# A list scheduler's cost table is rewritten, with a resource shared by VectorE and GpSimd

## The chip, the core and the metric

The program runs on one core of a Trainium2 chip. The metric is the device time of one execution in microseconds. TensorE multiplies matrices, VectorE (DVE in the profile), ScalarE (ACT) and GpSimd (POOL) do the elementwise work, and SyncE (SP) issues the DMAs. SBUF is the on-chip memory of all of them; PSUM holds TensorE's results and is not read by GpSimd.

## What is computed

Banded attention with a few sink columns, and behind it two feed-forward layers without residuals, all in float32. Shapes: 4 batch elements, 8 heads, 768 positions, 64 per head; 3072 tokens, d_model 512, d_ff 2048.

```
scores = scale * q @ k^T;  keep = (pos_k < n_sink) | (0 <= pos_q - pos_k < window)   # 4 and 128
a = softmax(where(keep, scores, -1e9)) ; x = (a @ v) as (tokens, 512)
h = relu(x @ w_in);      x = (h * h) @ w_out            # first layer
h = x @ w2_in;           y = (h - tanh(h)) @ w2_out     # second layer
```

The weights arrive as float64 words.

## The kernel before

Every float32 operand of a product is split into a high part, rounded to the type that TensorE multiplies fast, and a low part, the rest; a product is three fast ones (high by high, high by low, low by high). A split is a copy that rounds, on ScalarE or VectorE (`copy`, L200), and a subtraction, on VectorE or GpSimd (`sub`, L211). The subtraction reads two tensors in SBUF.

The work has these parts. Attention runs by jobs, a head's half of the queries, eight to a block of 384 tokens (`scores` L258, `values` L350; the jobs of blocks 0 and 1 are `plain`, L390, in float32 products without splits). Each weight half-chunk of 512 columns is loaded and turned from float64 to a high and a low float32 part (`w_split`, L485): a rescaling on ScalarE or VectorE (L500, L502), a shift (L509) and two bit merges (L511, L513) on VectorE, a rounding copy, a subtraction. The first layer (`step1`, L546) goes over 8 blocks of 384 tokens and 16 chunks of d_ff: a product into the PSUM bank `ph` (L527), relu (L557), square (L563), split, and the product into four accumulating banks (L541). The second (`step2`, L578) goes over 6 blocks of 512 tokens with a longer elementwise chain (L583 to L596) and two banks, `ph` and `S`, in turns, and accumulates at L543. The second layer's 32 weight halves take the places of the first layer's as these come free in its last block; `y_in` (L608) reads the first layer's result back from memory.

The order of the instructions is not written by hand. Each operation is added with the engines that may run it and a duration on each (`add`, L83), a due time by which operations are ranked, and the buffers that it reads and writes. `solve` (L102) then walks through model time. It takes the engine that is free first, goes through the operations ready on it, most urgent first, and gives it the first one that no other engine permitted for it would end earlier:

```
if all(max(free[g], op.ready.get(g, 0.0)) + queue(g, item) + op.engs[g] * self.WEIGH[g] >= now + op.engs[e] * self.WEIGH[e]
       for g in op.engs if g != e):
```

`queue` is the model time of the more urgent operations that are ready on the other engine, each divided by the number of engines that may run it. `WEIGH` counts VectorE's durations twice. The table `HOP` holds the wait from an operation's end to the start of one that needs it, by pairs of engines. The durations come from `c_act`, `c_dve`, `c_copy`, `c_sub` and `c_mm` (L168 to L186). At the end the operations are emitted in the order of their model starts; on the chip every engine runs its own in that order, and waits at the head of its queue for what the next one needs.

Of the kernel before, what the change touches and what calls it, by code (L numbers as in the profile page):

```python
# [38 lines left out]
PLAIN = 2 * H          # jobs (a head's half of the queries) in float32 products, those of the first batch element  # L39
# [4 lines left out]
# h - tanh(h) where u = h^2 < 1/64: h u (c0 + c1 u + c2 u^2) = h u ((s u + b)^2 + d), to float32's accuracy  # L44
# [17 lines left out]
# ---------------------------------------------------------------- order of the instructions  # L62
class Op:
    __slots__ = ("engs", "prio", "emit", "left", "out", "ready", "start", "eng", "lat")


class Order:
    """Places operations on the engines: what is ready, most urgent first, on the engine that ends it first.

    Operations are added in an order that is right when run one after the other; what one has to wait for  # L70
    follows from the buffers that it reads and writes."""

    # from an operation's end on one engine to the start of one on another that waits for it
    HOP = {"TV": 200.0, "TA": 200.0, "AV": 131.0, "VV": 127.0, "PV": 180.0, "VA": 128.0, "AA": 143.0, "PA": 169.0, "AP": 165.0, "VP": 155.0,
           "PP": 75.0, "AT": 217.0, "VT": 256.0, "PT": 200.0, "TP": 200.0, "VD": 500.0, "AD": 500.0, "TD": 500.0, "PD": 500.0}
    AHEAD = {"V": 900.0, "D": 1050.0}
    TICK, FIRST = 3413.0, 4590.0
    WEIGH = {"V": 2.0, "A": 1.0, "P": 1.0}
# [4 lines left out]
    def add(self, engs, prio, reads, writes, emit, lat=0.0):  # L83
        op = Op()
        op.engs, op.prio, op.emit, op.left, op.out, op.ready, op.eng, op.lat = engs, prio, emit, 0, [], {}, None, lat
# [15 lines left out]

    def solve(self):  # L102
# [3 lines left out]
        tick = {int(self.FIRST // self.TICK): self.TICK}  # L106

# [8 lines left out]
        def queue(g, item):  # L116
            return sum(i[2].engs[g] / len(i[2].engs) for i in avail[g] if i < item and i[2].eng is None)

        def cost(op, e, now):
            c = op.engs[e]  # L120
            if e == "T":    # TensorE's clock is halved after a tick in which it had little to do
                n = int((self.FIRST + now) // self.TICK)
                t = c if tick.get(n - 1, 0.0) >= 0.375 * self.TICK else 2.0 * c
                tick[n] = tick.get(n, 0.0) + c
                return t
            return c

        done, n = [], len(self.ops)
        while len(done) < n:
# [6 lines left out]
            best, skipped = None, []  # L136
# [18 lines left out]
            best.eng, best.start = e, now  # L155
            free[e] = now + cost(best, e, now)
            done.append(best)
            for d in best.out:
                for g in d.engs:
                    d.ready[g] = max(d.ready.get(g, 0.0), free[e] + self.HOP.get(e + g, 0.0) + best.lat)  # L160
# [4 lines left out]
        return max(free.values())  # L165
# [12 lines left out]


def c_sub(n):  # L180
    return {"V": c_dve(n), "P": 2.1 * n + 150}


def c_mm(n):
    return n / 2.4 + 1


class Fast:
    """The banded path, 0 <= n_sink <= 4 and 1 <= window <= 128: each query's window is one block of 128 columns,
    the later keys of the block before it and the earlier ones of its own, and 4 sink columns."""  # L190
# [8 lines left out]
    # one operation each; get() gives its operands when it is placed  # L199
# [11 lines left out]
    def sub(self, prio, reads, writes, get, n):  # L211
# [5 lines left out]
        self.o.add(c_sub(n), prio, reads, writes, emit)  # L217

    def load(self, prio, writes, get, nbytes, reads=()):
# [796 lines left out]
```

## Time and profile before

| | |
|---|---|
| device time, median of 3 runs | 1319.19 us (1318.81 to 1319.56) |
| span of the profiled execution | 1319.0 us |
| TensorE busy | 1267.7 us, 96% |
| VectorE busy | 1043.0 us, 79%, 2227 instructions |
| ScalarE busy | 749.8 us, 57%, 1909 instructions |
| GpSimd busy | 393.1 us, 30%, 511 instructions |

The span reaches from the program's first instruction to its last, and the profile page gives no other time for that execution; it lies within the range of the runs. TensorE's busy time counts pipelined matmuls whose ends are modelled, so its share overstates it. A wait at TensorE is booked either at the matmul (PE) or at the load of its weights (PEld).

### The profile page before, as it was taken

To read this page: it belongs to the slowest core of one execution; us is meant where nothing else is said; L and a number is where in the kernel's file an instruction comes from. 1 tells how busy PE (TensorE), PEld (TensorE's weight loads), DVE (VectorE), ACT (ScalarE), POOL (GpSimd) and SP (SyncE) were. 2 spreads that over 40 slices of the span, in tenths; PEclk is the share of its full clock that TensorE was granted. 3 is DMA by queue.
4 is the path that set the end of the run, shared out by engine and by line. 5 is a ranking of instruction groups with operands and counts; after the bars stand their busy time and mean duration, and the time that the engine had idled before them with its cause. 6 is when DMAs were issued, how large, how long until landed. Compare 5 with 4: busy or idle time off the path is not lost. (4 is left out here: it accounts for less than half of the span.)

```text
span 1319.0 us, 19532 instructions
## 1 busy us (share of the span) xinstructions
PE 1267.7 (96%) x6696; PEld 1120.9 (85%) x6696; DVE 1043.0 (79%) x2227; ACT 749.8 (57%) x1909; POOL 393.1 (30%) x511
## 2 busy tenths in 40 slices
PE   8889899999999999999998899999999999999998
PEld 5578799999999999999998777788888888888886
DVE  6899977888787888778848999886777776777665
ACT  5666566766677666776655555454444444544443
POOL 3466344455433555334534544100000000000000
PEclk9999999999999999999999999999999999999999
DMA  7773112221222212112018740010100100000000
GB/s 231 257 257 132 50 60 80 70 70 50 73 63 66 83 50 67 58 59 82 29 41 284 226 143 1 1 65 0 33 32 1 56 8 1 33 0 0 33 0 35
DMA packets 41723, 94.99 MB, mean 72 GB/s; under 512 B 4752, under 2 KB 18576, under 8 KB 41616
## 3 DMA queue, kind: packets, MB, share of 16 engines
q1 hardware_dynamic: 41472, 93.27, 21.7%
q8 instruction: 54, 0.88, 0.3%
q14 instruction: 53, 0.43, 0.1%
q10 hardware_dynamic: 144, 0.40, 0.1%
HBM read 79.50 MB, written 14.16 MB: 71 GB/s over the span
## 5 line engine op out<-in xcount | busy, mean ns | idle before, releaser
L527 PE MATMUL ph<-xh,w 128*128 128x384 f32 x1024 | 296.9, 341 | 8.7 <-ACT r L557 6.2
L541 PE MATMUL acc<-gh,w 128*128 128x384 f32 x1024 | 301.6, 345 | 0.3 <-ACT y L206 0.2
L543 PE MATMUL acc<-w,g2h 128*128 128x512 f32 x768 | 258.5, 396 | 0.0
L527 PEld LDWEIGHTS ph<-xh,w 128*128 128x128 f32 x1024 | 188.8, 189 | 13.9 <-ACT r L557 9.4
L541 PEld LDWEIGHTS acc<-gh,w 128*128 128x128 f32 x1024 | 188.3, 188 | 2.2 <-issue 0.9
L541 PE MATMUL acc<-gl,w 128*128 128x384 f32 x512 | 175.0, 342 | 7.4 <-DVE gl L216 3.9
L527 PE MATMUL ph<-xl,w 128*128 128x384 f32 x512 | 173.1, 338 | 2.0 <-DVE xl L216 1.8
L543 PEld LDWEIGHTS acc<-w,g2h 128*128 128x128 f32 x768 | 144.6, 188 | 34.0
L206 ACT CAST g2h<-r 128x512 fp32r<-128x512 f32 x94 | 58.3, 620 | 201.9 <-DVE r L596 201.8
L543 PE MATMUL acc<-w,g2l 128*128 128x512 f32 x384 | 152.6, 397 | 2.1 <-DVE g2l L216 1.1
L330 POOL TENSOR_SCALAR_AFFINE_SELECT pt<-xe 128x256 fp32r<-128x256 f32 (+1 forms) x192 | 92.8, 508 | 132.8 <-ACT xe L206 122.9
L527 PE MATMUL ph<-x2h,w 128*128 128x512 f32 x384 | 128.8, 394 | 3.3 <-DVE w L594 3.1
L527 PE MATMUL S<-x2h,w 128*128 128x512 f32 x384 | 127.8, 391 | 0.4 <-DVE w L594 0.4
L216 DVE TENSOR_TENSOR g2l<-r,g2h 128x512 fp32r<-128x512 f32 x90 | 62.2, 691 | 60.8 <-ACT g2h L206 60.8
L541 PEld LDWEIGHTS acc<-gl,w 128*128 128x128 f32 x512 | 96.2, 188 | 14.1 <-POOL gl L216 7.8
L284 ACT ACTIVATE cb<-cb,nm 128x132 f32<-128x132 f32 x144 | 58.6, 407 | 78.8 <-DVE nm L341 78.6
L216 POOL TENSOR_TENSOR x2l<-raw,x2h 128x512 fp32r<-128x512 f32 x12 | 17.4, 1449 | 285.3 <-ACT x2h L206 176.5
L527 PEld LDWEIGHTS ph<-xl,w 128*128 128x128 f32 x512 | 96.8, 189 | 4.0 <-DVE xl L216 3.7
L543 PEld LDWEIGHTS acc<-w,g2l 128*128 128x128 f32 x384 | 72.3, 188 | 21.3 <-DVE g2l L216 2.3
L527 PEld LDWEIGHTS ph<-x2h,w 128*128 128x128 f32 x384 | 72.6, 189 | 20.7 <-DVE w L594 3.9
L557 ACT ACTIVATE r<-ph 128x384 f32<-128x384 f32 x128 | 62.5, 488 | 46.2 <-PE ph L527 44.4
L590 DVE TENSOR_SCALAR mk<-u 128x512 uint8<-128x512 f32 x96 | 45.3, 472 | 54.3 <-ACT u L583 54.3
(189 smaller groups left out, 2768.3 us busy)
## 6 DMA issues: line engine op xcount, KB each, us to landing
wr<-w SPq DMA_DIRECT2D x64, 512.0 KB, 5.1
raw<-raw SPq DMA_DIRECT2D x32, 454.0 KB, 3.3
raw<-raw SPq DMA_DIRECT2D x31, 388.0 KB, 3.1
yd<-y SPq DMA_DIRECT2D x40, 192.0 KB, 2.5
raw<-yd SPq DMA_DIRECT2D x28, 256.0 KB, 2.9
out<-y SPq DMA_DIRECT2D x20, 256.0 KB, 2.0
raw<-raw SPq DMA_DIRECT2D x24, 160.0 KB, 2.9
raw<-raw SPq DMA_DIRECT2D x24, 128.0 KB, 2.2
```

Of the source, the lines that this page charges most:

```text
L206: nc.scalar.copy(out=out, in_=in_)
L216: (nc.vector if e == "V" else nc.gpsimd).tensor_tensor(out=out, in0=a, in1=b.bitcast(F32), op=ALU.subtract)
L284: lambda e, i=i: nc.scalar.activation(out=t[cb][:, i, :], in_=t[cb][:, i, :], func=AF.Exp, bias=t[nm][:, i:i + 1], scale=-1.0, accum_out=t ...
L330: lambda e, u=u, n=n, s=s, sign=sign, op=op: nc.gpsimd.affine_select(out=slots(u, n, s), in_=t[xe][:, 2 * u:2 * (u + n), :], pattern=[[0, ...
L527: nc.tensor.matmul(out=ph[:, :N], lhsT=w[:, a + c * P:a + (c + 1) * P], rhs=b[:, c, :], start=(c == 0 and k == 0), stop=(c == NE - 1 and k ...
L541: nc.tensor.matmul(out=acc[:, :N1], lhsT=w[:, a + e_ * P:a + (e_ + 1) * P], rhs=g, start=st, stop=sp)
L543: nc.tensor.matmul(out=acc, lhsT=g[:, e_ * P:(e_ + 1) * P], rhs=w[:, a:a + 512], start=st, stop=sp)
L557: nc.scalar.activation(out=r, in_=ph, func=AF.Relu)
L590: lambda e: nc.vector.tensor_scalar(out=T[mk], in0=T[u], scalar1=U_MAX, scalar2=None, op0=ALU.is_lt))
```

## The change

No instruction is added or removed; operations may go to another permitted engine or to another place in the order. Due times stay as they are. Comments are removed.

A duration becomes a triple `C(occ, took, port)`: how long the engine is occupied, how long until the result is there, and whether the operation needs the resource that VectorE and GpSimd share. All of GpSimd's operations need it, and of VectorE's those on SBUF alone; those that read PSUM don't. The weight of 2 on VectorE goes. The hops shrink, since they now count from `took`. Where the engine is ready earlier than the shared resource, the operation is held, and one of lower urgency may go first if it ends in time.

```diff
-    HOP = {"TV": 200.0, "TA": 200.0, "AV": 131.0, "VV": 127.0, "PV": 180.0, "VA": 128.0, "AA": 143.0, "PA": 169.0, "AP": 165.0, "VP": 155.0,
-           "PP": 75.0, "AT": 217.0, "VT": 256.0, "PT": 200.0, "TP": 200.0, "VD": 500.0, "AD": 500.0, "TD": 500.0, "PD": 500.0}
-    AHEAD = {"V": 900.0, "D": 1050.0}
+    HOP = {"TV": 40.0, "TA": 45.0, "AV": 35.0, "VV": 35.0, "PV": 40.0, "VA": 40.0, "AA": 35.0, "PA": 36.0, "AP": 75.0, "VP": 95.0,
+           "PP": 350.0, "AT": 55.0, "VT": 56.0, "PT": 56.0, "TP": 60.0, "TT": -160.0}
+    AHEAD = {"V": 1100.0, "D": 400.0}
-    WEIGH = {"V": 2.0, "A": 1.0, "P": 1.0}
+    NEAR = 60.0
...
+        def begin(op, e, now):
+            return max(now, port - 60.0) if op.engs[e][2] else now
...
-                if all(max(free[g], op.ready.get(g, 0.0)) + queue(g, item) + op.engs[g] * self.WEIGH[g] >= now + op.engs[e] * self.WEIGH[e]
+                at = begin(op, e, now)
+                if all(max(free[g], op.ready.get(g, 0.0), port if op.engs[g][2] else 0.0) + queue(g, item) + op.engs[g][1] >= at + op.engs[e][1]
                        for g in op.engs if g != e):
-                    best = op
-                    break
+                    if at <= now + self.NEAR:
+                        if held is None or now + op.engs[e][0] <= held[0] + self.NEAR:
+                            best = op
+                            break
+                    elif held is None:
+                        held = (at, item)
+                        continue
                 skipped.append(item)
...
+            if best.engs[e][2]:
+                port = max(port, at + occ)
...
 def c_act(n, psum=False, ptr=0):
-    return n / 1.2 + (51 if psum else 93) + 93 * ptr
-def c_dve(n, fast=False, ptr=0):
-    return n / (1.92 if fast else 0.96) + 70 + 60 * ptr
+    return C(n / 1.2 + (48 if psum else 98) + 92 * ptr, n / 1.2 + (162 if psum else 194) + 92 * ptr)
+def c_one(n, psum=False):
+    return C(n / 0.96 + 70) if psum else C(n / 1.92 + 70, None, True)      # None: took = occ + 85
+def c_two(n, psum=False):
+    return C(n / 0.96 + 72, None, not psum)
 def c_copy(n, psum=False):
-    return {"A": c_act(n, psum), "V": c_dve(n, not psum)}
-def c_sub(n):
-    return {"V": c_dve(n), "P": 2.1 * n + 150}
-def c_mm(n):
-    return n / 2.4 + 1
+    return {"A": c_act(n, psum), "V": c_one(n, psum)}
+def c_pool(n):
+    return C(2.35 * n + 110, 2.35 * n + 115, True)
+def c_sel(n):
+    return C(0.89 * n + 130, 0.89 * n + 180, True)
+def c_mm(*ns, slow=1):
+    t = sum(slow * (n * 0.4355 + 6.0) for n in ns)
+    return C(t, t + 165.0)
...
-        self.o.add({"D": max(nbytes / 360.0, 480.0)}, prio, reads, writes, emit, lat=2200.0)
+        t = max(nbytes / 300.0, 430.0)
+        self.o.add({"D": C(t, t + 1700.0)}, prio, reads, writes, emit)
```

A subtraction's durations are now `c_two` on VectorE and `c_pool` on GpSimd; the rescaling of weights costs ScalarE `c_act(568)`; the normalization of a job costs GpSimd 950 ns; the row minimum costs VectorE 222 ns and 375 ns to its result; the float32 products of `plain` take `slow=1.85`.

## Rows read from the trace of the kernel before

**Rows 1.** Page, busy tenths of two engines in 40 slices of the span

```profile
PE   8889899999999999999998899999999999999998
DVE  6899977888787888778848999886777776777665
```

**Rows 2.** Windows: bounds and length, each engine's busy time (instructions), clock, DMA

```profile
0.00:30.00 30.00, 24.33 (x101) 15.35 (x102) 19.50 (x100) 16.57 (x67) 10.66 (x26) 1.00 0.70 230
30.00:180.00 150.00, 131.40 (x715) 111.33 (x714) 142.02 (x318) 94.77 (x272) 77.47 (x81) 0.98 0.50 165
180.00:690.00 510.00, 504.88 (x3208) 497.33 (x3208) 396.54 (x1085) 343.26 (x1049) 230.81 (x353) 1.00 0.20 61
690.00:840.00 150.00, 133.85 (x633) 112.70 (x632) 142.92 (x202) 79.80 (x146) 62.84 (x43) 0.99 0.45 149
840.00:1319.00 479.00, 473.22 (x2048) 384.16 (x2046) 342.04 (x526) 215.40 (x377) 11.32 (x8) 1.00 0.06 21
```

**Rows 3.** Windows, the same columns (PE PEld DVE ACT POOL), two shorter stretches

```profile
60.00:150.00 90.00, 79.95 (x443) 68.73 (x444) 88.17 (x181) 55.17 (x147) 48.43 (x48) 1.00 0.51 172
720.00:840.00 120.00, 107.04 (x486) 87.78 (x487) 118.09 (x168) 63.17 (x115) 52.75 (x36) 0.99 0.34 113
```

**Rows 4.** Waits of PEld, 30 to 180 us: total, times, longest

```profile
PEld S L409 <- DVE pcb L417: 7.1, 9, 1.5
PEld O L471 <- POOL ppp L464: 6.6, 6, 2.5
```

**Rows 5.** Waits of PEld, 690 to 840 us

```profile
PEld ph L527 <- ACT r L557: 8.8, 10, 2.0
```

**Rows 6.** Timeline of VectorE near 740 us: start, duration, instruction

```profile
739.41 1.50 DVE L216 TENSOR_TENSOR w<-wd,w 128x512 fp32r<-128x512 f32 x1
740.84 1.78 DVE L513 SCALAR_TENSOR_TENSOR wd<-wr,wd 128x512 int32<-128x512 int32 x1
742.55 0.41 DVE L509 TENSOR_SCALAR wd<-wd 128x512 int32<-128x512 int32 x1
```

**Rows 7.** Timeline of GpSimd in the same stretch

```profile
738.98 1.40 POOL L216 TENSOR_TENSOR gl<-r,gh 128x384 fp32r<-128x384 f32 x1 [3.01 <-DVE gh L208]
740.33 1.74 POOL L216 TENSOR_TENSOR x2l<-raw,x2h 128x512 fp32r<-128x512 f32 x1
```

**Rows 8.** Source view of single lines, whole run: duration ns least/median/most

```profile
L513 DVE SCALAR_TENSOR_TENSOR wd<-wr,wd x64: 654/688/1782, 24.3 to 836.3; 128x512 int32<-128x512 int32 x64
L216 DVE TENSOR_TENSOR w<-wd,w x26: 677/692/1667, 46.4 to 837.7; 128x512 fp32r<-128x512 f32 x26
L216 DVE TENSOR_TENSOR gl<-r,gh x97: 535/558/1524, 61.2 to 747.4; 128x384 fp32r<-128x384 f32 x97
```

**Rows 9.** Lines by form, VectorE, 690 to 840 us: busy us, mean ns

```profile
L513 DVE SCALAR_TENSOR_TENSOR wd<-wr,wd 128x512 int32<-128x512 int32 x32 | 31.3, 977 | 0.4
L208 DVE CAST g2h<-r 128x512 fp32r<-128x512 f32 x2 | 2.0, 978 | 0.1
```

**Rows 10.** Lines by form, VectorE, 30 to 180 us

```profile
L513 DVE SCALAR_TENSOR_TENSOR wd<-wr,wd 128x512 int32<-128x512 int32 x31 | 27.5, 896 | 0.1
L441 DVE TENSOR_TENSOR psk<-pcb,prs 128x12 f32<-128x12 f32 x4 | 1.6, 406 | 0.0
```

**Rows 11.** Windows of line 216 (subtractions) alone: VectorE busy, GpSimd busy

```profile
30.00:180.00 150.00, 25.17 (x33) 50.13 (x38) 0.98 0.50 165
690.00:840.00 150.00, 23.34 (x28) 56.39 (x38) 0.99 0.45 149
```

**Rows 12.** Lines by form, ScalarE, 690 to 840 us; last column idle before, releaser

```profile
L500 ACT ACTIVATE wd<-wr 128x512 f32<-128x512 f32 x27 | 18.2, 676 | 24.4 <-DVE w L216 13.1 <-POOL w L216 8.3 <-DMA wr<-w 2.7
L206 ACT CAST w<-wd 128x512 fp32r<-128x512 f32 x27 | 16.6, 617 | 22.7 <-DVE wd L513 22.6
```

**Rows 13.** Timeline of VectorE near 868 us, GpSimd idle

```profile
868.48 0.69 DVE L216 TENSOR_TENSOR g2l<-r,g2h 128x512 fp32r<-128x512 f32 x1 [0.74 <-ACT g2h L206]
869.09 0.42 DVE L590 TENSOR_SCALAR mk<-u 128x512 uint8<-128x512 f32 x1
```

More of the change, by code (lines that the diff above doesn't have):

```diff
@@ L63, with __new__, times, add @@
 class Op:
-    __slots__ = ("engs", "prio", "emit", "left", "out", "ready", "start", "eng", "lat")
+    __slots__ = ("engs", "prio", "emit", "left", "out", "ready", "start", "eng", "end")
+class C(tuple):
+    def __new__(cls, occ, took=None, port=False):
+        return tuple.__new__(cls, (occ, occ + 85.0 if took is None else took, port))
+    def times(self, k):
+        return C(self[0] * k, self[0] * (k - 1) + self[1], self[2])
 class Order:
-    HOP = {"TV": 200.0, "TA": 200.0, "AV": 131.0, "VV": 127.0, "PV": 180.0, "VA": 128.0, "AA": 143.0, "PA": 169.0, "AP": 165.0, "VP": 155.0,
-           "PP": 75.0, "AT": 217.0, "VT": 256.0, "PT": 200.0, "TP": 200.0, "VD": 500.0, "AD": 500.0, "TD": 500.0, "PD": 500.0}
-    AHEAD = {"V": 900.0, "D": 1050.0}
+    HOP = {"TV": 40.0, "TA": 45.0, "AV": 35.0, "VV": 35.0, "PV": 40.0, "VA": 40.0, "AA": 35.0, "PA": 36.0, "AP": 75.0, "VP": 95.0,
+           "PP": 350.0, "AT": 55.0, "VT": 56.0, "PT": 56.0, "TP": 60.0, "TT": -160.0}
+    AHEAD = {"V": 1100.0, "D": 400.0}
     TICK, FIRST = 3413.0, 4590.0
-    WEIGH = {"V": 2.0, "A": 1.0, "P": 1.0}
+    NEAR = 60.0
     def __init__(self):
         self.ops, self.writer, self.readers = [], {}, {}
-    def add(self, engs, prio, reads, writes, emit, lat=0.0):
+    def add(self, engs, prio, reads, writes, emit):
         op = Op()
-        op.engs, op.prio, op.emit, op.left, op.out, op.ready, op.eng, op.lat = engs, prio, emit, 0, [], {}, None, lat
+        op.engs, op.prio, op.emit, op.left, op.out, op.ready, op.eng = engs, prio, emit, 0, [], {}, None
         deps = set()
@@ L116, in queue @@
         def queue(g, item):
-            return sum(i[2].engs[g] / len(i[2].engs) for i in avail[g] if i < item and i[2].eng is None)
+            return sum(i[2].engs[g][0] / len(i[2].engs) for i in avail[g] if i < item and i[2].eng is None)
         def cost(op, e, now):
@@ L135, in solve @@
                     heapq.heappush(avail[e], (op.prio, r, op))
-            best, skipped = None, []
+            best, held, skipped = None, None, []
             while avail[e]:
@@ L154, in solve @@
                 continue
-            best.eng, best.start = e, now
-            free[e] = now + cost(best, e, now)
+            at = begin(best, e, now)
+            occ, took = cost(best, e, at)
+            best.eng, best.start, best.end = e, at, at + took
+            free[e] = at + occ
+            if best.engs[e][2]:
+                port = max(port, at + occ)
             done.append(best)
@@ L159, in solve @@
                 for g in d.engs:
-                    d.ready[g] = max(d.ready.get(g, 0.0), free[e] + self.HOP.get(e + g, 0.0) + best.lat)
+                    d.ready[g] = max(d.ready.get(g, 0.0), best.end + self.hop(e, g))
                 d.left -= 1
@@ L286, in scores @@
         d = due[2]
-        o.add({"V": 73.0}, d - 9.9, [(*ss, i) for i in range(3)], [ss],
+        o.add({"V": c_one(3)}, d - 9.9, [(*ss, i) for i in range(3)], [ss],
               lambda e: nc.vector.tensor_scalar(out=t[ss], in0=t[ss], scalar1=1e-9, scalar2=None, op0=ALU.add))
-        o.add({"V": 80.0}, d - 9.8, [ss], [rs] + [(*ss, i) for i in range(3)], lambda e: nc.vector.reciprocal(out=t[rs], in_=t[ss]))
+        o.add({"V": C(95)}, d - 9.8, [ss], [rs] + [(*ss, i) for i in range(3)], lambda e: nc.vector.reciprocal(out=t[rs], in_=t[ss]))
         def norm(e):
@@ L328, in scores @@
             for s, sign, op in ((1, 1, ALU.is_ge), (0, -1, ALU.is_gt)):
-                o.add({"P": 0.91 * 2 * P * n + 128}, d - 5, [xk], [("pt", 2 * i + s) for i in range(u, u + n)],
+                o.add({"P": c_sel(2 * P * n)}, d - 5, [xk], [("pt", 2 * i + s) for i in range(u, u + n)],
                       lambda e, u=u, n=n, s=s, sign=sign, op=op: nc.gpsimd.affine_select(
@@ L339, in least @@
         m = self.c["m"][0 if half == 0 and i == 0 else 1 if half == 0 and i == 1 else 2]
-        self.o.add({"V": c_dve(132) + 8}, prio, [cb], [cb] + out,
+        self.o.add({"V": C(222, 375, True)}, prio, [cb], [cb] + out,
                    lambda e: nc.vector.tensor_tensor_reduce(out=get(), in0=get(), in1=m, op0=ALU.add, op1=ALU.min, scale=scale,
@@ L366, in pv @@
             nc.tensor.matmul(out=oo[:, :N1], lhsT=vv[:, 0, :], rhs=pts, start=False, stop=True)
-        o.add({"T": c_mm(N1) + (5 + 2 * half) * c_mm(256)}, d - 4,
+        o.add({"T": c_mm(N1, *[256] * (5 + 2 * half))}, d - 4,
               [("vh", k2), ("vl", k2)] + [("pts", k2, i) for i in range(3)] + [("pt", s) for s in range(1 - half, 6)], [ob], pv)
@@ L429, in plain @@
         d = due[2]
-        o.add({"V": 73.0}, d - 9.9, [(*ss, i) for i in range(3)], [ss],
+        o.add({"V": c_one(3)}, d - 9.9, [(*ss, i) for i in range(3)], [ss],
               lambda e: nc.vector.tensor_scalar(out=t[ss], in0=t[ss], scalar1=1e-9, scalar2=None, op0=ALU.add))
-        o.add({"V": 80.0}, d - 9.8, [ss], [rs] + [(*ss, i) for i in range(3)], lambda e: nc.vector.reciprocal(out=t[rs], in_=t[ss]))
+        o.add({"V": C(95)}, d - 9.8, [ss], [rs] + [(*ss, i) for i in range(3)], lambda e: nc.vector.reciprocal(out=t[rs], in_=t[ss]))
         def norm(w, out):
@@ L442, in norm @@
             return emit
-        o.add({"A": 3 * c_act(P, ptr=1), "V": c_dve(N1), "P": 2.1 * N1 + 150}, d - 9, [rs] + cbs, cbs, norm(slice(SK, 132), lambda: t[cb][:, :, SK:]))
-        o.add({"V": c_dve(3 * SK), "P": 2.1 * 3 * SK + 150}, d - 9, [rs] + cbs, [psk],
+        o.add({"A": c_act(P, ptr=1).times(3), "V": c_two(N1), "P": C(830, None, True)}, d - 9, [rs] + cbs, cbs, norm(slice(SK, 132), lambda: t[cb][:, :, SK:]))
+        o.add({"V": c_two(3 * SK), "P": C(260, None, True)}, d - 9, [rs] + cbs, [psk],
               norm(slice(0, SK), lambda: t[psk].rearrange("p (n s) -> p n s", s=32)[:, :, :SK]))
@@ L451, in tr @@
             nc.tensor.transpose(out=tt[0:96, 3 * P:4 * P], in_=t[psk], identity=self.c["idf"])
-        o.add({"T": 440.0}, d - 7, cbs + [psk], [tb], tr)
+        o.add({"T": c_mm(P, P, P, P, slow=1.75)}, d - 7, cbs + [psk], [tb], tr)
         if i0:
@@ L473, in pv @@
                 nc.tensor.matmul(out=out[:, i * P:(i + 1) * P], lhsT=v[0:96, (i - 1) % 3, :], rhs=t[ps][0:96, :], start=False, stop=(i == 2))
-        o.add({"T": 1000.0}, d - 4, [("rv", q), ps] + [(*pp, i) for i in range(3)], [ob], pv)
+        o.add({"T": c_mm(*[256] * (5 + 2 * half - 2 + half), *[P] * 6, slow=1.85)}, d - 4, [("rv", q), ps] + [(*pp, i) for i in range(3)], [ob], pv)
         self.copy(d - 3, [ob], [(*x, r)], lambda: (t[x][r:r + 64], bank[ob][r:r + 64, :N1]), N1, True)
```

78 lines of the change are left out of this document (44 added, 34 removed).

## The prediction

> **What bounds the kernel now.** Read the page's slices first: TensorE stands at 9 nearly everywhere, but dips at both ends of a long plateau, and just there VectorE stands at 8 and 9 [rows 1]. The windows by stage put numbers on it [rows 2]. From 180 to 690 us TensorE is busy 505 of 510 us, and from 840 on 473 of 479, the missing 6 lying behind the last product; no order of the elementwise work can win much there. From 30 to 180 and from 690 to 840, where weights are converted, it idles 18.6 and 16.2 us, and VectorE is busy 142.0 and 142.9 of 150. In the cores of these stages VectorE has no room left: 88.2 of 90 us and 118.1 of 120 [rows 3]. So two stages, 300 us together, are bound by VectorE, and the waits of TensorE's loads say through whom: in the first the masked scores of `plain` and GpSimd's selects come late [rows 4], in the second relu, which frees the bank `ph` [rows 5].
>
> But VectorE's busy time there isn't all work. At 739.41 a subtraction that alone takes 0.69 us (median, [rows 8]) took 1.50, ending 0.53 us after GpSimd's subtraction ended at 740.38; the merge behind it took 1.78 beside GpSimd's next one, and the shift after that is at its usual 0.41 [rows 6, 7]. Busy time of VectorE is here time spent held by GpSimd, and GpSimd's 1.40 and 1.74 are in part the reverse. The change's new resource describes that.
>
> The profiled span is 1319.0 us and the median 1319.19; I take the 0.2 us between them as what lies around the span and sum from 1319.2.
>
> **The change, part by part.** Nothing is added or removed, so each part is priced by which operations it sends elsewhere.
>
> *Subtractions from GpSimd to VectorE.* Before, a 512-wide one counted 2 x 603 = 1207 ns on VectorE and 1225 on GpSimd: GpSimd got it as soon as VectorE's backlog was 19 ns longer than its own. Now it counts 690 and 1318, and since the shared resource delays both alike, VectorE keeps it up to a backlog of some 630 ns (384 wide: 460). That is a strong push off GpSimd. What one is worth: in 690 to 840 us thirteen of VectorE's forms run above their undisturbed medians, the first L513 with 32 x (977 - 688) ns = 9.2 us, the last the rounding of g2h with 1.1 [rows 8, 9]; together 34 us, beside 62.8 us of GpSimd's work, so 0.54 us of VectorE for each us of it. In 30 to 180 us sixteen forms, first L513 with 31 x (896 - 688) ns = 6.4 us, last the small scaling of psk with 1.0 [rows 8, 10], give 40 us beside 77.5, so 0.51. A subtraction on GpSimd takes 56.39/38 = 1.48 us in the later stage and 50.13/38 = 1.32 in the earlier [rows 11]; it costs VectorE 0.80 and 0.67 us. On VectorE it costs its median less the 0.08 us by which the next instruction starts before its end [rows 13]: 0.61 us for 512 columns, 0.47 for 384 [rows 8], on average 0.57 and 0.54 with the widths of each stage. So a moved one gains 0.23 and 0.13 us, and all 76 of them 8.7 + 4.9 = 13.6. With a queue always standing at VectorE the planner will still pass the 630 ns often; I take half: **-7 us**. From both sides: L513 alone gives 9.2/38 = 0.24 us held per subtraction, by which a moved one loses 0.33 and half of them 13 us; the two of [rows 6] lost (1.50 - 0.69) + (1.78 - 0.69) = 1.90, so 0.95 each, by which all 76 gain 30. I stand by the sums over all forms, since they hold all of the excess.
>
> The trace and the Trainium skill differ on the 0.08 us. "VectorE: DVE Perf Modes", section "The DRAIN you can't avoid", says that the next VectorE instruction doesn't start until the pipe of the one before is empty; a later section of the page lets an instruction that isn't held start earlier. By the first, a moved subtraction would cost its full 0.69 us, half of them would gain 3 us less, and the table's `occ` would be 85 ns short on every VectorE instruction. Here 868.48 + 0.69 = 869.17, and the next one starts at 869.09 [rows 13], so I keep the overlap.
>
> *Roundings from ScalarE to VectorE.* The weight of 2 held these off VectorE: 673 ns against ScalarE's 520. Now 422 stand against 621, and for the rescaling of weights 422 against 667, so VectorE takes one up to a backlog of 199 or 245 ns. It has far more than that where it is bound, which limits the harm, but ScalarE is idle there for 24.4 and 22.7 us before these very operations, waiting for VectorE's chain [rows 12], and at such moments the backlog can be short. Each costs VectorE about its shift's 0.41 less 0.08, 0.33 us. There are 54 of the two kinds on ScalarE in 690 to 840 us [rows 12], and I take nine of those and of the earlier stage's: **+3 us**. Ends: a result 0.2 us earlier at each of nine links of the chain gains 2; all 54 lose 18, and with no more than as many in the earlier stage 36.
>
> *Durations to the result, hops, and holding.* In the model GpSimd's work now delays VectorE as it does on the chip, so a relu is less often queued on ScalarE behind a rounding whose input is late. The waits on this are 8.8 us at `ph`, and 6.6 and 7.1 at the selects and scores [rows 4, 5]: 22.5 us. I take a quarter, as part goes with the first term: **-5.5 us**; ends: none gained and as many lost again as taken, or all 22.5.
>
> *TensorE's and the DMAs' figures, the heads' start.* A 384-wide product counts 173 instead of 161 ns, loads 430 to 1748 instead of 480 to 1456. TensorE's and SyncE's own order follows the due times, which don't change; DMA is at half its share or less in these stages [rows 2]. Zero, hidden by the plateau of TensorE; the first 30 us, where TensorE idles 5.7, can move 2 either way. In 180 to 690 us GpSimd's normalizations also lean to VectorE, at 397 of 510 us; TensorE's 5 idle us there are the most to be won, and I give the plateau 0, plus or minus 5.
>
> Sum: 1319.2 - 7 + 3 - 5.5 = 1309.7, rounded to **1310 us**.
>
> **Rivals.** *Roundings swamp VectorE.* If the planner sends most of the roundings and rescalings over, say 72 of the 108 at most, VectorE gets 72 x 0.33 = 24 us in stages where it is the chain, against 12.5 gained: 1319 + 11 = **1330**. It decides from about 38 moved. For: a preference turned round by some 350 ns, and VectorE already full. Against: its backlog is counted before each choice. Chance 0.22.
>
> *No net change.* In a standing queue GpSimd keeps its subtractions, since 630 ns is one waiting merge, and what is gained by holding is lost again elsewhere: **1319**, within 2.6. For: 98% busy means that a queue is nearly always there. Against: the model now books VectorE as held, so it plans with less idle time. Chance 0.13.
>
> *The waits nearly vanish.* With all of the 13.6 us and two thirds of the 22.5, and three us of roundings: 1319.2 - 13.6 - 15 + 3 = **1294**. For: nothing but order stands behind those waits. Against: a greedy planner doesn't look ahead. Chance 0.13.
>
> *VectorE's instructions don't overlap.* If each holds the engine for its full duration, 38 moved subtractions cost 38 x 0.08 = 3 us more: **1313**. The start at 869.09 speaks against it [rows 13]. Chance 0.02. (It is the first of the two sections of the Trainium skill's page weighed above that would have it so.)
>
> **Numbers.** The forecast has 0.50, with its own range 1300 to 1316. About 0.2%, 2.6 us, is what a measurement of this kernel can tell from no change. Faster: 0.50 + 0.13 + 0.02 = 0.65, less 0.02 for a forecast that ends short of 2.6 us; same 0.13 + 0.02; slower 0.22. The range is 1290 to 1327: the lower end lies past the case of vanishing waits, the upper takes in the rounding case up to some 60 moved, and leaves out its worst.
>
> **What would show it.** Right: GpSimd's line 216 falls from 38 instructions in each of the two stages to about 19; L513's mean falls from 977 and 896 towards 690; VectorE stays near full in both stages, which end some 4 to 8 us earlier each; relu's wait at `ph` falls below 7; from 840 us on nothing changes but its start. Wrong: ScalarE's roundings and rescalings falling by more than a third there, with VectorE at 150 of 150; GpSimd's count unchanged; or new waits of TensorE between 180 and 690 us beyond 5.

## The result, and the profile after

The changed kernel takes 1297.99 us (median of 4 runs, 1297.06 to 1300.17) beside 1319.38 for the kernel before on the same chip: ratio 0.9843 [0.9831, 0.9854], or 21.4 us less. The forecast was 9 less. The sign was right, and so were the two stages where time is won; the size was not, and the runs below show that this net is made of larger terms of both signs.

The page of the changed kernel, busy time of each engine with its instructions, and the slices that answer to [rows 1]:

```profile
PE 1263.2 (97%) x6696; PEld 1115.6 (86%) x6696; DVE 1054.7 (81%) x2550; ACT 674.6 (52%) x1723; POOL 184.7 (14%) x332
...
PE   8999999999999999999999999999999999999997
...
DVE  6899998877878777878768999977877877877775
```

GpSimd gave up 179 of its 511 instructions and ScalarE 186 of 1909. TensorE's dips at the two ends of the plateau are gone from the slices. The windows of [rows 2], columns PE PEld DVE ACT POOL, for the changed kernel:

```profile
0.00:30.00 30.00, 24.17 (x106) 15.62 (x106) 19.68 (x107) 16.36 (x70) 5.43 (x19) 0.94 0.66 213
30.00:180.00 150.00, 145.66 (x856) 131.44 (x856) 142.60 (x387) 108.08 (x310) 43.74 (x58) 1.00 0.53 178
180.00:690.00 510.00, 498.32 (x3109) 479.04 (x3108) 398.95 (x1226) 307.99 (x915) 123.12 (x245) 1.00 0.22 64
690.00:840.00 150.00, 145.40 (x697) 126.84 (x696) 142.16 (x259) 86.10 (x154) 12.37 (x10) 0.99 0.41 135
840.00:1297.00 457.00, 449.64 (x1934) 362.70 (x1932) 351.27 (x577) 156.10 (x276) 0.00 (x0) 1.00 0.06 20
```

Read the counts of products here, not the busy times. Both kernels run the same 6696 products, so the window in which more of them were done shows where time was gained. From 30 to 180 us 856 were done instead of 715: 141 more, at 0.19 us each (the mean of 150/715 and 150/856), are 27 us gained. From 690 to 840 us 64 more at 0.226 are 14.5. But from 180 to 690 us 99 *fewer* were done, at 0.1615 us 16 lost, and from 840 on the products left take 0.236 us each instead of 0.234, 4.7 lost. With 1.4 for the head that is 27.1 + 1.4 - 16.0 + 14.5 - 4.7 = 22.3, and the spans differ by 1319.0 - 1296.8 = 22.2. (Products differ in width, so each term may be off by a few us; two products on a window's border count twice.) So the two stages bound by VectorE gave 42, and the stretches that I had put at zero took 21 back.

In the two stages the subtractions left GpSimd. Windows of line 267 alone (line 216 before), VectorE and GpSimd, to set beside [rows 11]:

```profile
30.00:180.00 150.00, 42.04 (x65) 16.91 (x17) 1.00 0.53 178
690.00:840.00 150.00, 43.01 (x64) 6.97 (x5) 0.99 0.41 135
```

From 38 and 38 to 17 and 5. And VectorE is held far less; the merge of L513, now L565, by form, 690 to 840 us and then 30 to 180 (busy us, mean ns), beside 977 and 896 [rows 9, 10]:

```profile
L565 DVE SCALAR_TENSOR_TENSOR wd<-wr,wd 128x512 int32<-128x512 int32 x31 | 22.2, 717 | 0.0
...
L565 DVE SCALAR_TENSOR_TENSOR wd<-wr,wd 128x512 int32<-128x512 int32 x31 | 22.6, 731 | 0.0
```

(The upper is the earlier stage's.) An estimate over all forms: taken over every instruction of VectorE, its time above the median that its form has beside an idle GpSimd was 40.5 us in 30 to 180 and 34.8 in 690 to 840; it is 15.2 and 4.4 after. TensorE's idle time in these stages falls from 18.6 and 16.2 us to 4.3 and 4.6. Waits of PEld, 30 to 180 and then 690 to 840 us (total, times, longest), beside [rows 4, 5]:

```profile
PEld O L523 <- POOL ppp L516: 1.5, 2, 1.2
PEld S L461 <- DVE pcb L469: 1.3, 2, 0.8
...
PEld ph L579 <- ACT r L609: 2.9, 3, 1.5
```

The 22.5 us of waits that the prediction added up are 5.7. In their place stand waits in the plateau. PEld, 180 to 690 us, the largest of the kernel before and then those of the changed kernel:

```profile
PEld acc L541 <- POOL gl L216: 3.8, 8, 0.5
...
PEld S L323 <- DVE cb L332: 12.5, 21, 0.8
PEld T L368 <- DVE a L267: 6.6, 12, 0.7
PEld acc L593 <- DVE gl L267: 3.9, 12, 0.7
```

The prediction had named this as a sign that it was wrong: new waits of TensorE between 180 and 690 us beyond 5.

### The profile page after: what moved, and what is told of

Its sections match the earlier page's. It is cut to its first block, busy times and chain, and to the rows that moved or that the text cites. A ratio compares the mean times of both kernels' runs of the same rounds, so it can differ in the third digit from the quotient of the medians.

```text
span 1296.8 us, 19460 instructions
## 1 busy us (share of the span) xinstructions
PE 1263.2 (97%) x6696; PEld 1115.6 (86%) x6696; DVE 1054.7 (81%) x2550; ACT 674.6 (52%) x1723; POOL 184.7 (14%) x332
## 4 chain that ended last, share of the span: by engine, by line
PE 75%; DVE 16%; ACT 4%; issue 3%; DMA 1%; POOL 1%; SPq 0%; DVEq 0%; ACTq 0%; POOLq 0%
PE ph L579 22%; PE acc L595 21%; PE acc L593 12%; PE S L579 10%; PE O L416 2%; PE T L368 2%; PE O L523 1%; PE S L323 1%; DVE xl L267 1%; DVE cb L332 1%; DVE x L429 1%; DVE qq L267 1%; DVE gl L267 1%; PE S L461 1%; DMA raw<-yd 1%
## 5 line engine op out<-in xcount | busy, mean ns | idle before, releaser
L579 PE MATMUL ph<-xh,w 128*128 128x384 f32 x1024 | 337.9, 342 | 2.9 <-ACT r L609 2.6
L593 PE MATMUL acc<-gh,w 128*128 128x384 f32 x1024 | 315.2, 342 | 0.0
L595 PE MATMUL acc<-w,g2h 128*128 128x512 f32 x768 | 301.6, 396 | 1.0 <-DVE g2h L259 1.0
L579 PE MATMUL ph<-x2h,w 128*128 128x512 f32 x384 | 150.2, 394 | 2.7 <-DVE w L646 2.7
L579 PE MATMUL S<-x2h,w 128*128 128x512 f32 x384 | 149.4, 390 | 0.0
L635 ACT ACTIVATE u<-ph 128x512 f32<-128x512 f32 x48 | 28.7, 597 | 157.3 <-PE ph L579 157.3
L642 DVE TENSOR_SCALAR mk<-u 128x512 uint8<-128x512 f32 x96 | 41.5, 432 | 74.6 <-ACT u L635 74.6
L267 DVE TENSOR_TENSOR gl<-r,gh 128x384 fp32r<-128x384 f32 x123 | 69.3, 564 | 36.6 <-ACT gh L257 35.9
L635 ACT ACTIVATE u<-S 128x512 f32<-128x512 f32 x48 | 28.7, 598 | 130.4 <-PE S L579 130.1
L579 PEld LDWEIGHTS S<-x2h,w 128*128 128x128 f32 x384 | 72.2, 188 | 16.5
```

The costliest lines, as they stand in the source:

```text
L267: (nc.vector if e == "V" else nc.gpsimd).tensor_tensor(out=out, in0=a, in1=b.bitcast(F32), op=ALU.subtract)
L579: nc.tensor.matmul(out=ph[:, :N], lhsT=w[:, a + c * P:a + (c + 1) * P], rhs=b[:, c, :], start=(c == 0 and k == 0), stop=(c == NE - 1 and k ...
L593: nc.tensor.matmul(out=acc[:, :N1], lhsT=w[:, a + e_ * P:a + (e_ + 1) * P], rhs=g, start=st, stop=sp)
L595: nc.tensor.matmul(out=acc, lhsT=g[:, e_ * P:(e_ + 1) * P], rhs=w[:, a:a + 512], start=st, stop=sp)
L635: o.add({"A": c_act(N2, True)}, v + 1.5, [pb], [u], lambda e: nc.scalar.activation(out=T[u], in_=self.bank[pb], func=AF.Square))
L642: lambda e: nc.vector.tensor_scalar(out=T[mk], in0=T[u], scalar1=U_MAX, scalar2=None, op0=ALU.is_lt))
```

## The experiments

Each was timed in three rounds beside the kernel before. "After" is the changed kernel.

| run | what it is | median us | ratio to before |
|---|---|---|---|
| e1_no_port | after, nothing needs the shared resource | 1326.2 | 1.006 [1.0038, 1.0083] |
| e2_before_subs_v | before, no subtraction on GpSimd | 1274.1 | 0.9657 [0.9641, 0.9673] |
| e3_copies_act | after, roundings count on VectorE twice | 1293.5 | 0.9809 [0.9793, 0.9825] |
| e4_old_mm | after, TensorE's old durations | 1297.3 | 0.9839 [0.9823, 0.9855] |
| e5_slack_T | after, results for TensorE due 250 ns earlier | 1313.7 | 0.9962 [0.9948, 0.9976] |
| e6_after_subs_v | after, no two-input arithmetic of `c_pool` on GpSimd | 1300.2 | 0.9857 [0.9840, 0.9873] |
| e7_before_no_weight | before, VectorE's weight 1 | 1308.9 | 0.9915 [0.9899, 0.9932] |
| e8_before_pool_selects | e2, normalizations and additions off GpSimd too | 1269.1 | 0.9620 [0.9603, 0.9638] |
| e9_subs_v_no_weight | e2 and e7 together | 1309.6 | 0.9927 [0.9911, 0.9944] |
| e10_after_subs_v_weight2 | e6, VectorE weighed 2 | 1295.2 | 0.9816 [0.9796, 0.9835] |
| e11_after_weight2 | after, VectorE weighed 2 | 1303.0 | 0.9884 [0.9864, 0.9904] |
| e12_after_tt | after, next product of a sum ready in time | 1279.4 | 0.9698 [0.9682, 0.9714] |
| e13_after_subs_v_weight2_tt | e10 and e12 together | 1266.3 | 0.9597 [0.9581, 0.9613] |
| e14_before_subs_v_tt | e2, next product of a sum 5 ns late | 1289.0 | 0.9773 [0.9757, 0.9789] |
| e15_after_pool_selects_weight2_tt | e13, normalizations off GpSimd | 1268.1 | 0.9614 [0.9598, 0.9630] |
| e16_after_tt_no_port | e12 without the resource | 1310.0 | 0.9933 [0.9917, 0.9950] |
| e17_subs_v_weight2_tt_no_port | e13 without the resource | 1275.3 | 0.9667 [0.9651, 0.9683] |

### The subtractions and the resource

**e1** takes the resource out of the new table, **e2** puts the ban on GpSimd's subtractions into the old one (and on a small addition, L379, that uses the same line and stood on GpSimd 22 times).

```diff
-        return tuple.__new__(cls, (occ, occ + 85.0 if took is None else took, port))    # e1, in C
+        return tuple.__new__(cls, (occ, occ + 85.0 if took is None else took, False))
-    return {"V": c_dve(n), "P": 2.1 * n + 150}                                          # e2, in c_sub of before
+    return {"V": c_dve(n)}
```

> The changed kernel, but the planner knows of no shared resource (no operation needs it); durations, hops and the missing weight stay. Theory H (the gain is VectorE's time that GpSimd no longer holds, part by subtractions moved over, part by placing what is left on GpSimd beside VectorE's PSUM work): VectorE's instructions are stretched again, L565 (the old L513) to a mean above 800 ns from 688 in 690 to 840 us, and some 8 us are lost: 1306. Theory D (the gain is from true durations and waits, through roundings that end earlier on VectorE and a better order): 1298 within 3, with the stretching back but off the path.

> The kernel before with one edit: subtractions and small additions of c_sub may run on VectorE alone; its table, hops and weight of 2 stay. Theory H: the two stages bound by VectorE lose most of their 74 us of stretching and pay some 45 us of subtractions, so 10 to 20 us are gained: 1304. Theory D: VectorE only gets more work where it is full: 1319 or slower, up to 1335.

e2: one line gives 45 us, twice what the whole change gives. Its windows of 30 to 180, 180 to 690 and 690 to 840 us:

```profile
30.00:180.00 150.00, 142.64 (x816) 127.24 (x815) 131.17 (x364) 106.18 (x304) 40.98 (x59) 0.98 0.52 169
180.00:690.00 510.00, 508.72 (x3237) 503.81 (x3236) 388.73 (x1181) 358.02 (x1078) 123.00 (x214) 1.00 0.24 75
690.00:840.00 150.00, 149.03 (x698) 127.28 (x699) 142.25 (x255) 94.45 (x170) 5.27 (x4) 1.00 0.34 111
```

101 and 65 products more in the two stages than before [rows 2], and 29 more, not fewer, in the plateau. VectorE does all 38 + 38 subtractions more and yet is busy 131 instead of 142 of 150 us in the first stage: what it was held for was more than the work that it took over.

e1: without the resource the new table is slower than the old one, by 7 us, though it leaves nearly as few subtractions on GpSimd (18 and 7 in the two stages, after: 17 and 5). The stretching that theory H expected did not come: L565 has a mean of 696 and 684 ns there. So the resource gives 28 us, and neither through the subtractions of these stages nor through time that VectorE is held in them. What it moves most are copies. Windows of the copies on VectorE (line 259, which rounds or only copies out of PSUM), 30 to 180, 180 to 690 and 690 to 840 us, first e1:

```profile
30.00:180.00 150.00, 28.30 (x76) 0.99 0.52 173
180.00:690.00 510.00, 146.54 (x371) 1.00 0.20 60
690.00:840.00 150.00, 8.24 (x18) 0.99 0.45 146
```

and the changed kernel:

```profile
30.00:180.00 150.00, 20.23 (x50) 1.00 0.53 178
180.00:690.00 510.00, 119.55 (x315) 1.00 0.22 64
690.00:840.00 150.00, 5.13 (x13) 0.99 0.41 135
```

In e1 VectorE has 87 copies more in these 810 us, some 56 of them roundings. With the resource the model sees VectorE as held and leaves them to ScalarE. That these copies are the 28 us is argued, since no run moves them alone.

e1's time is close to that of the rival that the roundings swamp VectorE (1330 forecast, 1326 measured), but by luck, since its mechanism is not there. Of what the rival counted, the roundings and rescalings of weights, VectorE has 37 in the two stages against 31 before; it wanted 38 more. And both stages do more products than before, 52 and 80, while the plateau does 144 fewer. Part of that is the order of TensorE's products, which comes below.

**e6** takes the arithmetic that is left from GpSimd (`"P": c_pool(...)` gone from the subtraction, the square and two additions).

> The changed kernel, but subtractions, the square and the small additions may run on VectorE alone. The kernel before with only such an edit took 1274, 24 us less than the change. Theory L (the 24 us are the subtractions that the change still leaves on GpSimd): 1274 to 1282. Theory R (they are the price of the rest of the new table): 1293 to 1300.

1300.2, no gain: GpSimd's remaining subtractions are not what keeps the changed kernel 24 us behind e2.

### The weight

**e3** counts a rounding's VectorE time twice in the new table; **e7** and **e9** set `WEIGH["V"]` to 1 in the old one, with and without GpSimd's subtractions.

```diff
-    return {"A": c_act(n, psum), "V": c_one(n, psum)}                   # e3, in c_copy
+    v = c_one(n, psum)
+    return {"A": c_act(n, psum), "V": C(v[0], v[1] + v[0], v[2])}
-    WEIGH = {"V": 2.0, "A": 1.0, "P": 1.0}                              # e7, e9
+    WEIGH = {"V": 1.0, "A": 1.0, "P": 1.0}
```

> The changed kernel, but where a rounding or copy is weighed between ScalarE and VectorE, VectorE's time counts twice, as before; everything else stays. If roundings on VectorE are a price of the change (my term of +3 us): VectorE's full stages get shorter, 1293 to 1297. If they are part of the gain (a result 0.2 us earlier in each link of the weights' chain, theory D): 1301 to 1306. Instructions on VectorE fall from 2550 towards 2300.

> The kernel before with the weight of VectorE at 1 instead of 2, nothing else. Subtractions then go to GpSimd from a backlog of 622 ns on VectorE instead of 19, and roundings turn to VectorE (337 against 520 ns). Theory S (moving subtractions is the gain, whatever moves them): GpSimd's line 216 falls by half or more, 1290 to 1305. Theory C (the roundings that come along cost as much): 1312 to 1330, with VectorE above 2500 instructions.

> The kernel before with subtractions on VectorE alone and its weight at 1 instead of 2: against the same with weight 2 (1274) it shows the roundings that turn to VectorE, by themselves. Theory C (they cost): 1284 to 1295 and VectorE above 2550 instructions from 2377. If they don't matter, since the backlog is counted: 1274 within 4.

e3 gains 4.5 us on after, as was expected if these copies are a price: VectorE has 2357 instructions instead of 2550.

The weight did two opposite things. It pushed subtractions to GpSimd: without it (e7) GpSimd has 339 instructions instead of 511, and the kernel is 10.5 us faster. And it kept copies on ScalarE: where no subtraction can go to GpSimd (e9 against e2), leaving it out costs 35 us. The plateau of e9:

```profile
180.00:690.00 510.00, 491.96 (x3080) 476.42 (x3079) 449.45 (x1394) 273.97 (x832) 122.08 (x182) 1.00 0.20 60
```

Against e2's row VectorE has 61 us more, ScalarE 84 less, and TensorE does 157 products fewer, 25 us at 0.16. So most of the harm falls in the plateau, where VectorE is not full. TensorE's largest wait of e9 there:

```profile
PEld O L364 <- POOL pt L330: 17.2, 22, 1.0
```

**e10** and **e11** bring a weight of 2 into the new comparison, with GpSimd's arithmetic banned and allowed.

```diff
-  ... + op.engs[g][1] >= at + op.engs[e][1]
+  ... + op.engs[g][1] + op.engs[g][0] * (g == "V") >= at + op.engs[e][1] + op.engs[e][0] * (e == "V")
```

> The changed kernel with subtractions on VectorE alone (1300) and VectorE's time counted twice again wherever engines are compared; durations, hops and the shared resource are the new ones. Theory W (the missing weight is the whole price of the rest of the table): 1268 to 1278, TensorE's waits from 180 to 690 us below 8 from 23.6, VectorE below 390 us there. If hops, durations or holding cost too: 1284 to 1296.

> The changed kernel with VectorE's time counted twice again, subtractions free to go to GpSimd: a 512-wide one counts 1295 against 1318 ns, so GpSimd gets it from a backlog of 23 ns, as before, but the planner knows the shared resource. If knowing it is enough to place them where they hold nobody: 1270 to 1285. If subtractions on GpSimd cost whatever the planner knows: GpSimd above 300 us, VectorE's L565 stretched above 800 ns, 1295 to 1315.

e11 is slower than after: the weight sends subtractions back (GpSimd 628 instructions, the mean of L565 971 ns from 690 to 840 us), though the resource is counted. e10 gains 5 only, and its plateau says why something else is at work:

```profile
180.00:690.00 510.00, 497.52 (x3108) 480.23 (x3108) 340.14 (x1119) 385.06 (x1128) 86.19 (x178) 1.00 0.22 66
```

VectorE and ScalarE have room, 340 and 385 of 510 us, and still TensorE does 3108 products, no more than after; its loads wait for one thing above all:

```profile
PEld ph L579 <- ACT r L609: 19.9, 33, 1.0
```

### TensorE's own order

**e4** puts TensorE's old durations into the new table, **e5** makes the model deliver to TensorE 250 ns later, so that elementwise work is done earlier.

```diff
-    t = sum(slow * (n * 0.4355 + 6.0) for n in ns)                      # e4
+    t = sum(slow * (n / 2.4 + 1.0) for n in ns)
-           ... "AT": 55.0, "VT": 56.0, "PT": 56.0, ...                  # e5
+           ... "AT": 305.0, "VT": 306.0, "PT": 306.0, ...
```

> The changed kernel with the old time of a product in the planner (n/2.4 + 1 ns instead of 0.4355 n + 6; the 165 ns to the result stay). Theory T (a planner that takes TensorE for 7% faster than it is leaves VectorE slack in front of each product, which the true figure takes away): the 14 us that the middle gave back return, 1283 to 1290, and the waits of PEld at L323 and L368 (19.1 us) fall below 8. If TensorE's figure plays no part: 1298 within 4.

> The changed kernel with 250 ns more in the planner's hop from VectorE, ScalarE and GpSimd to TensorE, nothing else. Between 180 and 690 us the changed kernel gives back 14 us, at waits of TensorE for scores' copies (L332) and for the parts of the probabilities (L267). Theory P (the planner, now true in TensorE's own time, puts products just where their input is due, and the chip is late by some 0.3 us): the middle regains most of it, the waits at L323 and L368 fall from 19 us to under 6, total 1286 to 1291. Theory V (VectorE, at 399 of 510 us there, is itself too full after the move of subtractions): the waits stay and the total is 1297 to 1303.

e4 changes nothing in total, though its plateau does 48 products more and the two stages 31 fewer. e5 was to cure the plateau's waits if hops too short had made them; it cost 16 us, and my theory that they had fell with it.

The timelines show the cause. TensorE from 351.05 us in the changed kernel (start, duration):

```profile
351.05 0.34 PE L579 MATMUL ph<-xh,w 128*128 128x384 f32 x1
351.22 0.34 PE L579 MATMUL ph<-xl,w 128*128 128x384 f32 x1
351.40 0.34 PE L579 MATMUL ph<-xh,w 128*128 128x384 f32 x1
351.57 0.34 PE L593 MATMUL acc<-gh,w 128*128 128x384 f32 x1
351.75 0.33 PE L593 MATMUL acc<-gl,w 128*128 128x384 f32 x1
351.93 0.33 PE L593 MATMUL acc<-gh,w 128*128 128x384 f32 x1
352.10 0.33 PE L579 MATMUL ph<-xh,w 128*128 128x384 f32 x1
```

Three products of one sum, three of another, and back. In the kernel before a sum's twelve products stand in one piece:

```profile
351.96 0.33 PE L541 MATMUL acc<-gh,w 128*128 128x384 f32 x1
...
353.87 0.34 PE L541 MATMUL acc<-gh,w 128*128 128x384 f32 x1
354.05 0.34 PE L527 MATMUL ph<-xh,w 128*128 128x384 f32 x1
...
355.96 0.34 PE L527 MATMUL ph<-xh,w 128*128 128x384 f32 x1
```

It follows from the table: a product's result comes `occ` + 165 ns after its start and the hop `TT` is -160, so the next chunk of three of the same sum is ready 5 ns after TensorE is free, and at that moment the planner, which ranks only what is ready, takes another sum's. Two sums side by side each end late, and relu, which frees `ph`, comes late with them. **e12** makes the next chunk ready 5 ns early, **e14** makes it 5 ns late in e2's old table.

```diff
-    ... "TP": 60.0, "TT": -160.0}            # e12, and with e10's edits e13
+    ... "TP": 60.0, "TT": -170.0}
-    "PP": 75.0, "AT": 217.0, ...             # e14, on e2
+    "PP": 75.0, "TT": 5.0, "AT": 217.0, ...
```

> The changed kernel with one number of its table other: the hop from TensorE to TensorE at -170 instead of -160 ns. With 165 ns to a product's result, -160 makes the next chunk of the same sum ready 5 ns after TensorE is free, so the planner takes another sum's chunk in between, and the trace shows sums in alternating threes where the kernel before has runs of twelve. Theory G (the alternation spreads each sum over twice the time, so relu and all behind it have half of it left): runs of twelve return, PEld's waits from 180 to 690 us fall from 30 to under 10 and the last 4 us at the end come back: 1275 to 1288. If the order of sums plays no part: 1298 within 4.

> The other way round: the kernel before with subtractions on VectorE alone (1274) and a hop of 5 ns from TensorE to TensorE, where its table had none. Theory G: sums alternate, TensorE waits between 180 and 690 us and 4 us go at the end: 1285 to 1300. Otherwise 1274 within 3.

> As above, with subtractions on VectorE alone and its time counted twice (1295 without the new hop). Theory G: the 21 us to the kernel before with subtractions on VectorE (1274) are the alternation: 1266 to 1276. Otherwise 1290 to 1297.

e12 gains 19 us on after, e14 loses 15 on e2, and e13 gains 29 on e10, its pair: ten nanoseconds in one number. e12's timeline has the whole sums again:

```profile
350.37 0.33 PE L579 MATMUL ph<-xh,w 128*128 128x384 f32 x1
...
352.27 0.34 PE L579 MATMUL ph<-xh,w 128*128 128x384 f32 x1
352.45 0.28 PE L323 MATMUL S<-kh,qq 128*128 128x260 f32 x1
```

and its plateau, and that of e14 below, have the products that were missing or miss those that e2 has:

```profile
180.00:690.00 510.00, 505.36 (x3180) 493.60 (x3179) 425.32 (x1258) 315.05 (x926) 128.04 (x238) 1.00 0.23 71
```

```profile
180.00:690.00 510.00, 506.67 (x3170) 492.12 (x3169) 361.62 (x1155) 367.02 (x1094) 115.04 (x201) 1.00 0.24 72
```

71 more than after, 67 fewer than e2; at 0.16 us some 11 of the 19 and of the 15. The rest lies in other stretches and is not followed here. TensorE's loads wait 15.1 us in e12's plateau in place of 27.6, so not under 10, as was expected: the waits at L323 and L368 for `cb` and `a` are nearly gone, but 9.6 us stand at L368 for `xe`. That a sum spread out is late by its length is argued; that the alternation costs is shown.

e13, 1266.3 us (1264.9 to 1267.5), beats both kernels, by 53 and 32 us. TensorE's largest wait in its plateau is 1.7 us:

```profile
PEld ph L579 <- DVE xl L267: 1.7, 3, 0.6
```

### What is left, and the resource again

**e8** and **e15** also take the normalizations from GpSimd (e8 the additions of the second layer's input too); **e16** and **e17** repeat e1's edit on e12 and e13.

> The kernel before with subtractions on VectorE alone (1274), and now its normalizations and the additions of y_in off GpSimd too, so that GpSimd has only selects. If each microsecond on GpSimd costs VectorE what it did before: 1268 to 1273, most of it before 180 us, where TensorE still waits 18 us. If the normalizations, now on ScalarE and VectorE, are missed: 1275 to 1282.

> e13 with normalizations off GpSimd too. If the new durations are worth something once the hop, the weight and GpSimd's work are out of the way: under 1269, the best so far (the kernel before with only selects on GpSimd): 1260 to 1268. If they aren't: 1267 to 1275.

> The changed kernel with the hop from TensorE to TensorE at -170 (1279) and without the shared resource. In the alternating table the resource was worth 28 us (1298 against 1326). If it is worth that by itself: 1300 to 1310. If it only covered up what the alternation cost: 1279 to 1288.

> The best kernel (subtractions on VectorE, its time counted twice, the hop at -170: 1266), without the shared resource. If the resource works by keeping work off GpSimd and roundings off VectorE, which the ban and the weight do here already: 1266 within 4. If placing selects beside VectorE's PSUM work is worth something too: 1272 to 1282, with more stretching on VectorE.

In the old table GpSimd's last two-input work is worth 5 us more (e8); in the new one, where the resource is counted, it is worth nothing (e15: the medians are 1.9 us apart the other way, within their intervals). The resource gives 31 us with whole sums (e16 against e12) as it gave 28 without, and 9 even where GpSimd's arithmetic is banned and VectorE weighed (e17 against e13). And without the resource whole sums are worth 16 us (e16 against e1).

e16 shows what the resource does in the first stage, too. Its waits of PEld, 30 to 180 us, beside [rows 4]:

```profile
PEld O L523 <- POOL ppp L516: 7.0, 8, 2.1
PEld S L461 <- DVE pcb L469: 6.3, 12, 1.0
```

New durations and hops alone leave these as they were; in e12 they are 0.3 and 1.3 us.

## Why the prediction was wrong

The steps in their order, each against its measure.

- *Two stages are bound by VectorE, which is held by GpSimd*: right. e2 alone shows it, and VectorE remains full in both (142.6 and 142.2 of 150 us) while TensorE does 141 and 64 products more. That the stages would end 4 to 8 us earlier each was far too little.
- *The subtractions, -7 us*: **this step failed first**. 54 left the two stages, not 38, so "I take half" was low. And the price was low: all 76 were to gain 13.6 us, and e2, which moves them all, gains 101 and 65 products in the two stages, some 35 us. "0.54 us of VectorE for each us of it" spread what VectorE was held for over all of GpSimd's work: 0.80 and 0.67 us for a subtraction. In e2's first stage GpSimd is still busy 41 us with selects and normalizations, and VectorE's time above its medians is 9 us, not 40.5; so, as an estimate, the subtractions held some (40.5 - 9.0)/38 = 0.83 us each there, and by the same difference (34.8 - 1.5)/38 = 0.88 later. After, 40.5 + 34.8 - 15.2 - 4.4 = 55.7 us less are held, for 54 x 0.55 = 30 us of work taken over: -26 in place of -7.
- *Roundings, +3*: wrong in number and place. Of the two kinds that the term counts, VectorE has 34 in the two stages after and 31 before, three more and not nine; and where the cost shows is the plateau. There e7, which only drops the weight, does 124 products fewer than the kernel before, some 20 us at 0.16, while its two stages do 97 and 94 more. Weight gone, subtractions and roundings together, the forecast had -4; e7 measures -10.5.
- *Durations, hops and holding, -5.5*: **a failed step, and the largest in us**. 16.8 of the 22.5 us of waits are gone; a quarter was taken. Between e7 and e12 stand these three, with the figures of TensorE and the DMAs and the starts that were put at zero, and they measure -29.5 together. The durations and hops give nothing of it (e16 is 1.1 us slower than e7): it is the resource, which the prediction priced by these waits only. It takes copies off VectorE in the plateau as well (414 there in e16, 322 in e12).
- *TensorE's order, 0, plateau 0 plus or minus 5*: **a failed step of the other sign**. "TensorE's and SyncE's own order follows the due times, which don't change" is false: due times rank only what is ready, and the hop `TT` made the more urgent sum's next chunk unready by 5 ns. TensorE's row in the diff was read for its durations, which change nothing in total (e4), and not for its hop. (Nor do all hops shrink: `PP` grows from 75 to 350, and `TT` is new.) The plateau lost 16 us and the last stage 4.7; taking the alternation away gives 19 (e12).
- *VectorE's overlap*: the term for instructions that don't overlap has no place here either: in e2 a merge that starts at 109.50 us and lasts 0.68 is followed at 110.10.
- *From 840 only the start moves*: not quite. VectorE's copies there rise, and TensorE's loads now wait 1.5 us once for the rounding of g2h; the 4.7 us above are small beside the rest.

Of the rivals, the vanishing waits (1294) came nearest, and for the reason it gave: nothing but order stands behind those waits. It stands by accident, though: it has no lost plateau.

In all, the runs give a path from the kernel before to the changed one on which each step adds one part of the change:

| step | from, to | median us | step us | forecast |
|---|---|---|---|---|
| the weight goes | before, e7 | 1319.4, 1308.9 | -10.5 | -7 + 3 |
| new durations, hops and starts, without resource and alternation | e7, e16 | 1308.9, 1310.0 | +1.1 | in the next |
| the resource | e16, e12 | 1310.0, 1279.4 | -30.6 | -5.5 |
| sums in threes | e12, after | 1279.4, 1298.0 | +18.6 | 0 |

The steps sum to -21.4 by construction; what the path adds is where the forecast lost its us. In other places the resource gives -28 (after against e1) or -9 (e17, e13), the alternation +15 to +29, the missing weight -5 (after against e11), but +35 where subtractions are banned from GpSimd (e9 against e2). So the signs of resource and alternation hold, and the weight's depends on what it may move. Each kernel is one schedule of a greedy planner, and e4 shuffles tens of products between stages for nothing, so steps of a few us prove no cause. Open are the part of e2's 45 us that comes from shorter waits, as against a freer VectorE, how much of the resource's gain is copies and how much a better order, and why the weight is worth 5 us in e10 and 13 between e12 and e13, where the ban changes too.

## What to carry to other kernels

Where an engine off the critical chain shares a resource with the one on it, price what its instructions hold, by their kind, and not by its busy time: here two-input arithmetic held VectorE, and selects hardly did (in e8 they are nearly GpSimd's only work, 24.5 us in the first stage, and VectorE's time above its medians is some 5 us there). Compare stages by how many products were done in them, since busy time hid half of the loss. And in a list scheduler look at every number that decides a tie: ten nanoseconds in one hop moved 15 to 29 us, and a table's rows have to be tried one at a time, because a net of -21 was -10.5, +1, -31 and +19.

## What was not expected of the hardware

The holding goes both ways, and a queue of VectorE's instructions can starve GpSimd. In e2's trace a select that takes 0.98 us at 99.31 took 3.91 at 107.26. GpSimd, and then VectorE:

```profile
99.31 0.98 POOL L461 TENSOR_SCALAR_AFFINE_SELECT ppp<-pxe 128x384 f32<-128x384 f32 x1 [2.96 <-PE ph L527]
100.24 0.57 POOL L464 TENSOR_SCALAR_AFFINE_SELECT ppp<-pxe 128x384 f32<-128x384 f32 x1
...
107.26 3.91 POOL L461 TENSOR_SCALAR_AFFINE_SELECT ppp<-pxe 128x384 f32<-128x384 f32 x1 [3.96 <-ACT pxe L206]
```

```profile
100.37 0.99 DVE L513 SCALAR_TENSOR_TENSOR wd<-wr,wd 128x512 int32<-128x512 int32 x1
...
107.43 0.41 DVE L509 TENSOR_SCALAR wd<-wd 128x512 int32<-128x512 int32 x1
...
109.50 0.68 DVE L513 SCALAR_TENSOR_TENSOR wd<-wr,wd 128x512 int32<-128x512 int32 x1
110.10 0.68 DVE L511 SCALAR_TENSOR_TENSOR wd<-wr,wd 128x512 int32<-128x512 int32 x1
```

Seven of VectorE's instructions in a row from 107.43 us run at their usual durations, with one- and two-input ones among them, and the select ends at 111.17, 0.39 us after the last of them (110.10 + 0.68). The Trainium skill, "SBUF — State Buffer", section "SBUF: two separate sides", has an exclusive lock between GpSimd's operations and those of VectorE that use two ports or have two SBUF inputs: the first to start holds it for its whole instruction, while the other blocks. The trace agrees in that nobody runs at half speed, but here the select started first by the profile (107.26 against 107.43) and still it was the one that waited, and through seven instructions rather than one. (Spans on GpSimd are rough, so the 0.17 us between the starts may not be the order in which the two asked; that it was busy through seven stands.) It is no rule: at 100.24 a select took 0.57 us and the merge beside it 0.99 instead of 0.68, and of e2's 301 instructions on GpSimd three ran more than 0.9 us over the median of their form.
